# Moving a handful of vector steps, gaps and stores around in a fused attention and feed-forward kernel

## The chip, the cores and the metric

The kernel runs on one core of one Trainium2 chip. A core has five engines that run side by side, each through its own list of instructions in order: PE (TensorE, matrix products, with weight loads that overlap them), DVE (VectorE), ACT (ScalarE), POOL (GpSimd) and SP (SyncE, here only a queue that issues transfers). They meet at semaphores. The products land in PSUM, a small memory in banks which PE writes and DVE and ACT read; everything else on the chip lies in SBUF. The metric is the time of one execution on the device in microseconds (us), lower is better.

## The reference, cut to what matters

Two stages follow each other. The first is a linear attention with decay for 4 batches, 8 heads, 768 tokens and head size 64, in blocks of 64 tokens:

```python
for b in range(nb):                                  # 12 blocks of 64 tokens
    intra = einsum('bhic,bhjc->bhij', qb, kb) * Dmask
    intra = einsum('bhij,bhjd->bhid', intra, vb)
    inter = einsum('bhid,bhde->bhie', qb * lam_pow, kv_state)
    out[:, :, sl] = intra + inter
    kv_state = lam_block * kv_state + einsum('bhsd,bhse->bhde', kb * rev_pow, vb)
```

Its output, read as 3072 tokens of 512 features, goes through a feed-forward layer with an ELU:

```python
h = x @ w_in                                         # 512 -> 2048
g = where(h > 0, h, exp(minimum(h, 0)) - 1)
out = g @ w_out                                      # 2048 -> 512
```

## The kernel before, in words

**Blocks, groups, rounds.** Two batches by one block of 64 tokens make a *block* s of 128 rows; there are 24 (s = 0 to 23). Two blocks make a *group* of 256 rows; there are 12. The tile framework runs with a manual schedule: every engine's list is in the order in which the program writes the instructions, so the order of the Python text is the order of work. A string of words (`start`) writes out the first part, up to block 8 of the attention and group 2 of the feed-forward; then a loop runs *rounds* `grp` = 3 to 11, each of eight steps `u` = 0 to 7, and a written-out tail ends the program.

**One step of a round.** Step u calls `mm1_h` (L385): eight matmuls that give H(grp,u), a PSUM tile `psH` of two features blocks by 256 tokens. There are two such tiles (`bufs=2`), so H(grp,u) can start when the reader of the tile before the last has finished. Then, by step, come a *visit* to the attention (at u = 1 and 5), four matmuls of `mm2` for block 5 at four places (the list `five`), a *part* of the second product (below), small DVE and ACT work, and at the end `elu(grp,u)`, which turns H into `g` in float16.

**Two forms of the ELU.** In round 3 `mm1_e` and `mm1_g` are used: ACT reads the PSUM tile twice (exponential L395, Relu L397), which frees it, and DVE joins the two SBUF tiles (L402: both inputs in SBUF). In rounds 4 to 11 ACT makes the Relu of the negative (L429) and then its exponential from SBUF (L431), and DVE joins that with the PSUM tile itself (L432), which frees the tile.

**A visit.** `visit(s, ...)` puts out, in this order on PE, the first half of the products with the old state (L304), the scores of block s+1 (L328), the state update of block s (L320, which reads `vd` of block s), the other half with the state, the products with the scores (L313) and, for early blocks, transposes (L335). What it needs is made beforehand: `vd` of block s+1 by `decay_v` (L191, DVE, two SBUF inputs), at u = 3 and u = 6; `qs` and `sd` of block s+1 by `decay_q` (L209) and `decay_s` (L200), on DVE for early blocks and, from block 10 on, on POOL. POOL also issues all loads of q, k and v (L70), six to a block, in the same list.

**The second product.** Blocks 0 to 5 take 16 plain matmuls each (`mm2`, L452). From group 3 on a group is done by seven products of half size (`part`, L508), Strassen-like: they need sums of `g` (`g_sum`, L490) and four sums of quarters of `w_out`, the tiles `wt[1]` to `wt[4]` (`w_sum`, L478, half a tile a call). The parts go into two PSUM banks A and B; `keep` (L538, ACT) copies a bank's part out before it is written again, `add` (L542) and `c2` (L546) on DVE make the output tiles, and `store` (L527) issues two transfers for each, one for each batch, both on SP.

**Where the change touches.** In the tail the parts of group 11 use the two `psH` tiles as their banks, and the last four stores are: the first half of block 22 on SP, block 23 on SP, the second half of block 22 on ACT and SP.

Of the kernel before, what the change touches and what calls it, by code (L numbers as in the profile page):

```python
# [16 lines left out]
def kernel(  # L17
# [35 lines left out]
    def half(x):  # L53
        return slice(64 * x, 64 * x + 64)
# [365 lines left out]
    def elu(grp, u):  # L420

        psH, nb, T, name = unit[grp, 0, 2, u]
        if grp == 3:
            mm1_e(grp, 0, 2, u)
            mm1_g(grp, 0, 2, u, NF2)
            return

        r = msb.tile([128, nb, T], FP32, tag="r", bufs=4, name=f"r{name}")
        nc.scalar.activation(r[:], psH[:], AF.Relu, scale=-1.0)  # L429
        e = msb.tile([128, nb, T], FP32, tag="e", bufs=4, name=f"e{name}")  # L430
        nc.scalar.activation(e[:], r[:], AF.Exp, scale=-1.0)  # L431
        nc.vector.scalar_tensor_tensor(  # L432
            out=place(grp, 0, 2, u, 2, NF2), in0=e[:], scalar=-1.0, in1=psH[:],
            op0=ALU.add, op1=ALU.max,
        )
# [4 lines left out]
    def rows(s, r):  # L440

        b, c = where(s)
        r0 = (b + r) * S + c * L
        return out[r0 : r0 + L, :]


    def mm2(s, n0):
        if n0 == 0:
            acc[s] = M[nacc[0] % 2][:]
            nacc[0] += 1  # L450
        for n in range(n0, n0 + 4):
            nc.tensor.matmul(  # L452
                acc[s], lhsT=g_of(s, n), rhs=wo[n // 4][:, n % 4, :],
                start=(n == 0), stop=(n == NFT - 1),
            )
# [26 lines left out]
    def g_sum(grp, i):  # L482
        A = gel[grp]
        A11, A12, A21, A22 = (A[:, :, j, c * 128 : (c + 1) * 128] for c in range(2) for j in range(2))
        gs[grp, i] = msb.tile([128, NF2, 128], FP16, tag=f"s{i}", name=f"s{i}_{grp}")
        a, b = {
            1: lambda: (A21, A22), 2: lambda: (gs[grp, 1][:], A11), 3: lambda: (A11, A21),
            4: lambda: (A12, gs[grp, 2][:]),
        }[i]()
        nc.vector.tensor_tensor(  # L490
            out=gs[grp, i][:], in0=a, in1=b, op=ALU.add if i == 1 else ALU.subtract
        )
# [32 lines left out]
    def store(s, o, cols):  # L525
        for r in range(2):
            nc.sync.dma_start(out=rows(s, r)[:, cols], in_=o[half(r), cols])  # L527

    def out_tile(grp, c):
        d = res[grp]  # L530
# [10 lines left out]
        o = out_tile(grp, c)[:, cols]  # L541
        nc.vector.tensor_tensor(out=o, in0=src, in1=res[grp][kept][:], op=ALU.add)  # L542

    def c2(grp):
# [5 lines left out]
        store(2 * grp + 1, d[1], slice(0, DM))  # L550

    def consts(i):
        if i == 0:
# [42 lines left out]

    lo, hi = slice(0, HD), slice(HD, DM)

    sums = {(3, 4): 2, (4, 0): 4, (4, 3): 3}
    five = [(3, 2), (3, 5), (4, 0), (4, 2)]  # L600
    nload = 12
    for grp in range(3, NG):
        old, new = grp - 2, grp - 1
        for u in range(8):
            mm1_h(grp, 0, 2, u, NF2)
            s = 2 * grp + 2 + u // 4
            if s < NS and u % 4 == 0:

                if nload < NS:
                    load("k", nload)  # L610
                    load("q", nload)
                if nload <= NS:
                    load("v", nload - 1)
                    nload += 1
            if s < NS and u % 4 == 1:
                decay_q(s + 1, nc.vector if s < 9 else nc.gpsimd)
                decay_s(s + 1, nc.vector if s < 9 else nc.gpsimd)
                visit(
                    s, s if s < NS - NPR else None, s + 1 if s + 1 < NS else None,
                    s + 2 if s + 2 < NT else None,  # L620
                )
# [12 lines left out]
            if new >= 3 and u in (4, 5, 6, 7):
                g_sum(new, {4: 1, 5: 2, 6: 4, 7: 3}[u])
            if new >= 3 and u == 4:
                add(new, 0, lo, res[new]["A"][:, hi], "p2")
            if s + 1 < NS:
                if u % 4 == 1:
                    att_P(s + 1)  # L640
                if u % 4 == 2:
                    att_C(s + 2)
                    att_N(s)
                if u in (3, 6):
                    decay_v(s + 1, nc.vector)
# [46 lines left out]
    for r in range(2):  # L692
        (nc.scalar, nc.sync)[r].dma_start(out=rows(2 * G, r)[:, hi], in_=d[0][half(r), hi])


# [28 lines left out]
```

## Time and profile before

| | |
|---|---|
| runs shown | 214.62, 215.43 and 218.25 us; median 215.43 |
| profiled execution | 214.9 us; its span, from the first to the last instruction, 213.1 us |
| mean granted TensorE clock | 0.992 |
| PE busy | 191.2 us, 90% of the span, 3384 matmuls |
| DVE busy | 170.3 us, 80% |
| ACT busy | 141.6 us, 66% |
| POOL busy | 136.8 us, 64% |

Times within the profile are counted from the first instruction. Busy is the time in which at least one instruction of the engine runs; PE's matmuls overlap, so full rows of PE mean that matmuls follow each other without a gap, not that nothing could be quicker. A row of the timeline gives the start, the time from the first start to the last end, the line, the tile written and those read, the count and, in brackets, the idle time of the engine ahead of it with what ended it. DVE instructions that follow each other overlap by some 0.08 us, so a row of 0.68 us costs 0.60 us of the queue.

### The profile page before, as it was taken

Reading aid. Unit: us, or ns where it says so; the run is one execution under the profiler, and the core shown is the slowest. Engines: PE = TensorE matmul, PEld = TensorE weight load, DVE = VectorE, ACT = ScalarE, POOL = GpSimd, SP = SyncE. Lnnn points to the kernel's source line nnn. Section 1 sums busy time; section 2 is a strip of 40 time slices with the busy share of each in tenths; the row PEclk is TensorE's granted clock in tenths of the full one; section 3 lists DMA queues with packets and bytes.
Section 4 is the critical chain, followed back from the end, with each engine's and each line's share of the span. In section 5 each row is a group of like instructions: output and inputs, shape, how many; then the busy total and the mean of one; then the engine's idle time right before and its main releaser. Section 6 shows DMA issues by size and latency. Waiting matters only on the chain.

```text
span 213.1 us, 7908 instructions
## 1 busy us (share of the span) xinstructions
PE 191.2 (90%) x3384; PEld 158.3 (74%) x3384; DVE 170.3 (80%) x278; ACT 141.6 (66%) x265; POOL 136.8 (64%) x184
## 2 busy tenths in 40 slices
PE   0448989999999994899999999999999999999990
PEld 0347978648777763588888888888888888888880
DVE  3677895789997999897997997997979967757751
ACT  5314786724766874377868878778878788887620
POOL 8979832998999999997979979979522200000000
PEclk9999999999999999699999999999999999999999
DMA  6999999999999999997998999999923304013044
GB/s 103 142 151 157 170 201 184 180 126 163 124 140 124 116 148 105 105 105 81 130 171 78 144 164 65 137 132 119 161 42 73 80 3 101 3 24 75 3 98 98
DMA packets 98643, 24.11 MB, mean 113 GB/s; under 512 B 91312, under 2 KB 95664, under 8 KB 98608
## 3 DMA queue, kind: packets, MB, share of 16 engines
q0 software_dynamic: 78208, 13.38, 85.7%
q1 hardware_dynamic: 19120, 9.90, 25.9%
q10 hardware_dynamic: 1280, 0.33, 0.9%
q8 instruction: 26, 0.43, 0.8%
q14 instruction: 9, 0.07, 0.1%
HBM read 27.27 MB, written 6.29 MB: 157 GB/s over the span
## 4 chain that ended last, share of the span: by engine, by line
PE 80%; DVE 9%; POOL 3%; DMA 3%; ACT 1%; issue 1%; POOLq 0%; DVEq 0%
PE psH L385 37%; PE psM L508 23%; PE psM L452 9%; DVE g L402 3%; DMA wi<-in_moe_w_in_dram 3%; PE psO_None L304 2%; PE psZ L328 2%; POOL vn L70 1%; PE psHB L508 1%; PE psHA L508 1%; PE psO_None L313 1%; PE psZ L320 1%; DVE vd L191 1%; DVE wt L478 1%; DVE P L217 1%
## 5 line engine op out<-in xcount | busy, mean ns | idle before, releaser
L385 PE MATMUL psH<-xt,wi 128*128 128x256 f16 (+1 forms) x960 | 101.5, 256 | 6.8 <-DVE g L432 4.0
L385 PEld LDWEIGHTS <-wi 128*128 128x128 f16 x960 | 80.2, 100 | 18.3 <-issue 8.0
L432 DVE SCALAR_TENSOR_TENSOR g<-e,psH 128x512 f16<-128x512 f32 x64 | 43.8, 685 | 18.4 <-ACT e L431 17.8
L429 ACT ACTIVATE r<-psH 128x512 f32<-128x512 f32 x64 | 38.2, 597 | 25.7 <-PE psH L385 25.4
L431 ACT ACTIVATE e<-r 128x512 f32<-128x512 f32 x64 | 40.3, 630 | 2.0
L70 POOL DMA_DIRECT2D qn<-in_q_dram x46 | 32.3, 729 | 4.8 <-issue 4.4
L70 POOL DMA_DIRECT2D kn<-in_k_dram x46 | 32.6, 728 | 3.3 <-DMA wo<-in_moe_w_out_dram 2.5
L70 POOL DMA_DIRECT2D vn<-in_v_dram x48 | 34.2, 748 | 0.1
L395 ACT ACTIVATE e<-psH 128x512 f32<-128x512 f32 x32 | 19.2, 599 | 17.4 <-PE psH L385 17.3
L508 PEld LDWEIGHTS <-s 128*128 128x128 f16 x288 | 28.2, 98 | 3.3
L402 DVE SCALAR_TENSOR_TENSOR g<-e,r 128x512 f16<-128x512 f32 x32 | 24.4, 772 | 5.8 <-ACT r L397 5.8
L508 PE MATMUL psM<-wt,s 128*128 128x256 f16 x192 | 24.9, 273 | 0.0
L452 PE MATMUL psM<-wo,g 128*128 128x512 f16 x96 | 24.8, 390 | 0.0
L209 POOL TENSOR_TENSOR qs<-TD,powi 128x512 f16<-128x512 f16 x13 | 16.2, 1245 | 12.1 <-PE psO_None L304 12.1
L508 PEld LDWEIGHTS <-g 128*128 128x128 f16 x216 | 20.6, 98 | 2.7
L200 POOL TENSOR_TENSOR sd<-st,lamL 128x512 f32<-128x512 f16 x12 | 15.8, 1315 | 8.1 <-DVE st L264 8.1
L397 ACT ACTIVATE r<-psH 128x512 f16<-128x512 f32 x32 | 19.2, 599 | 0.0
L217 DVE TENSOR_TENSOR P<-psZ,mask 128x512 f16<-128x512 f32 x24 | 16.4, 685 | 2.5 <-PE psZ L328 2.2
L508 PE MATMUL psM<-wo,g 128*128 128x256 f16 x136 | 17.6, 273 | 0.0
L191 DVE TENSOR_TENSOR vd<-vn,rev 128x512 f16<-128x512 f16 x22 | 16.3, 739 | 0.1
L252 ACT CAST xt<-psO_None 128x512 f16<-128x512 f32 x19 | 10.9, 573 | 5.5 <-PE psO_None L313 5.5
L264 DVE TENSOR_TENSOR st<-psZ,sd 128x512 f16<-128x512 f32 x20 | 13.6, 681 | 0.9 <-PE psZ L320 0.9
(77 smaller groups left out, 209.0 us busy)
## 6 DMA issues: line engine op xcount, KB each, us to landing
out_dram<-o SPq DMA_DIRECT2D x46, 128.0 KB, 2.9
vn<-in_v_dram POOLq DMA_DIRECT2D x48, 64.0 KB, 4.5
kn<-in_k_dram POOLq DMA_DIRECT2D x46, 64.0 KB, 4.7
qn<-in_q_dram POOLq DMA_DIRECT2D x46, 64.0 KB, 3.4
wi<-in_moe_w_in_dram POOLq DMA_DIRECT2D x8, 256.0 KB, 6.0
wo<-in_moe_w_out_dram POOLq DMA_DIRECT2D x4, 512.0 KB, 11.3
kraw<-in_k_dram SPq DMA_DIRECT2D x2, 128.0 KB, 4.4
qraw<-in_q_dram ACTq DMA_DIRECT2D x2, 128.0 KB, 4.6
```

The costliest lines, as they stand in the source:

```text
L70: nc.gpsimd.dma_start(out=keep[s][half(r)], in_=src[b + r, :, c * L : (c + 1) * L, :].rearrange("h p d -> p h d"),)
L191: eng.tensor_tensor(out=st[s]["vd"][:], in0=vn[s][:], in1=rev[:].unsqueeze(2).broadcast_to([128, H, D]), op=ALU.mult,)
L217: nc.vector.tensor_tensor(out=d["P"][:].rearrange("p y j t -> p y (j t)"), in0=psS, in1=mask[:].rearrange("p y j t -> p y (j t)"), op=ALU. ...
L385: nc.tensor.matmul(psH[:, i, :], lhsT=wi[n // 4][:, kk, (n % 4) * 128 : (n % 4 + 1) * 128], rhs=xt[grp][:, kk, c0 * 128 : c0 * 128 + T], s ...
L395: nc.scalar.activation(e[:], psH[:], AF.Exp)
L397: nc.scalar.activation(r[:], psH[:], AF.Relu)
L402: nc.vector.scalar_tensor_tensor(out=place(grp, c0, nc_, n0, nb, step), in0=e[:], scalar=-1.0, in1=r[:], op0=ALU.add, op1=ALU.min,)
L429: nc.scalar.activation(r[:], psH[:], AF.Relu, scale=-1.0)
L431: nc.scalar.activation(e[:], r[:], AF.Exp, scale=-1.0)
L432: nc.vector.scalar_tensor_tensor(out=place(grp, 0, 2, u, 2, NF2), in0=e[:], scalar=-1.0, in1=psH[:], op0=ALU.add, op1=ALU.max,)
L452: nc.tensor.matmul(acc[s], lhsT=g_of(s, n), rhs=wo[n // 4][:, n % 4, :], start=(n == 0), stop=(n == NFT - 1),)
L508: nc.tensor.matmul(to, lhsT=lhsT, rhs=rhs, start=start and n == 0, stop=stop and n == NF2 - 1, skip_group_check=True,)
```

## The change

Six edits, in the program's order:

1. The two sums `wt[2]` and `wt[4]` (second halves) are made at the end of `start`, ahead of round 3, where before they stood at steps (3,4) and (4,0); that of `wt[3]` moves from step (4,3) to step (4,7).
2. Steps 6 and 7 of round 3 use the form of the ELU in which DVE reads PSUM; steps 0 to 5 keep the other.
3. In round 3, `vd` at u = 3 and u = 6 is made after that step's ELU instead of ahead of it.
4. The four pieces of block 5's second product stand at steps (3,2), (3,4), (3,6) and (4,0) instead of (3,2), (3,5), (4,0) and (4,2), and its copy and store with the last of them.
5. In round 11 the parts of group 10 stand at other steps (2, 4, 1, 5, 6, 3 at u = 1, 3, 4, 5, 6, 7), so that only part 7 is left for the tail; the copies and the sums of `g` that go with them move along, and the tail's `c2` of group 10 stands ahead of group 11's part 1.
6. The store of block 23 goes out on SP and ACT, one transfer each, instead of both on SP.

```diff
 def elu(grp, u):
-        if grp == 3:
+        if grp == 3 and u < 6:
...
-        "... A7.7.8.9 G2.1.1.8 M4.12 X7 N7 P8 Z4 C9 "
+        "... A7.7.8.9 G2.1.1.8 M4.12 X7 N7 P8 Z4 C9 B2.1 B4.1 "
...
-    sums = {(3, 4): 2, (4, 0): 4, (4, 3): 3}
-    five = [(3, 2), (3, 5), (4, 0), (4, 2)]
+    sums = {(4, 7): 3}
+    five = [(3, 2), (3, 4), (3, 6), (4, 0)]
...
-            if new >= 3 and u > 2:
-                part(new, {3: 2, 4: 1, 5: 4, 6: 5, 7: 6}[u])
+            if new >= 3:
+                at_u = {1: 2, 3: 4, 4: 1, 5: 5, 6: 6, 7: 3} if end else {3: 2, 4: 1, 5: 4, 6: 5, 7: 6}
+                if u in at_u:
+                    part(new, at_u[u])
...
-                if u in (3, 6):
+                if u in (3, 6) and grp > 3:
                     decay_v(s + 1, nc.vector)
...
             elu(grp, u)
+            if grp == 3 and u in (3, 6):
+                decay_v(s + 1, nc.vector)
...
+            if end and u == 6:
+                keep(new, "u2", res[new]["A"][:, hi], 1)
+            if end and u == 7:
+                add(new, 0, hi, res[new]["B"][:, hi], "u2")
+                store(2 * new, res[new][0], slice(0, DM))
...
-    keep(G, "u2", d["A"][:, hi], 1)
-    part(G, 3)
-    add(G, 0, hi, d["B"][:, hi], "u2")
-    store(2 * G, d[0], slice(0, DM))
     part(G, 7)
...
     g_sum(G, 1)
+    c2(G - 1)
     part(G, 1)
-    c2(G - 1)
...
-    c2(G)
+    c2(G, (nc.sync, nc.scalar))
```

More of the change, by code (lines that the diff above doesn't have):

```diff
@@ L523, in part, with store @@
         product_of(grp, i, d[bank][:, cols], first, i in (4, 2, 3, 7))
-    def store(s, o, cols):
+    def store(s, o, cols, queues=(nc.sync, nc.sync)):
         for r in range(2):
-            nc.sync.dma_start(out=rows(s, r)[:, cols], in_=o[half(r), cols])
+            queues[r].dma_start(out=rows(s, r)[:, cols], in_=o[half(r), cols])
     def out_tile(grp, c):
@@ L542, in add, with c2 @@
         nc.vector.tensor_tensor(out=o, in0=src, in1=res[grp][kept][:], op=ALU.add)
-    def c2(grp):
+    def c2(grp, queues=(nc.sync, nc.sync)):
         d = res[grp]
@@ L549, in c2 @@
         )
-        store(2 * grp + 1, d[1], slice(0, DM))
+        store(2 * grp + 1, d[1], slice(0, DM), queues)
     def consts(i):
@@ L625 @@
                 mm2(5, 4 * five.index((grp, u)))
+            end = grp == NG - 1
             if old >= 3 and u in (0, 2):
                 part(old, {0: 3, 2: 7}[u])
-            if new >= 3 and u > 2:
-                part(new, {3: 2, 4: 1, 5: 4, 6: 5, 7: 6}[u])
+            if new >= 3:
+                at_u = {1: 2, 3: 4, 4: 1, 5: 5, 6: 6, 7: 3} if end else {3: 2, 4: 1, 5: 4, 6: 5, 7: 6}
+                if u in at_u:
+                    part(new, at_u[u])
             if old >= 3 and u == 1:
@@ L633 @@
                 store(2 * old, res[old][0], slice(0, DM))
-            if new >= 3 and u in (4, 5, 6, 7):
-                g_sum(new, {4: 1, 5: 2, 6: 4, 7: 3}[u])
+            if new >= 3 and u in (4, 5, 6, 3 if end else 7):
+                g_sum(new, {4: 1, 5: 2, 6: 4}.get(u, 3))
             if new >= 3 and u == 4:
@@ L654 @@
                 keep(old, "p35", res[old]["B"][:, hi])
-            if new >= 3 and u == 3:
+            if new >= 3 and u == (1 if end else 3):
                 keep(new, "p2", res[new]["B"][:, lo])
-            if new >= 3 and u == 6:
+            if new >= 3 and u == (5 if end else 6):
                 keep(new, "c45", res[new]["B"][:])
+            if end and u == 6:
[3 more added lines that the diff above has]
+                store(2 * new, res[new][0], slice(0, DM))
             if (grp, u) == five[-1]:
@@ L688 @@
     part(G, 7)
-    c2(G)
+    c2(G, (nc.sync, nc.scalar))
     part(G, 3)
     add(G, 0, hi, HB[:, hi], "u2")
-    for r in range(2):
-        (nc.scalar, nc.sync)[r].dma_start(out=rows(2 * G, r)[:, hi], in_=d[0][half(r), hi])
+    store(2 * G, d[0], hi, (nc.scalar, nc.sync))
 _INS = ['q', 'k', 'v', 'lam', 'moe_w_in', 'moe_w_out']
```

2 rows, old and new, of the table start are left out of this document.

## The prediction

> **What bounds the kernel now.** First the page: who is busy.
>
> ```profile
> PE 191.2 (90%) x3384; PEld 158.3 (74%) x3384; DVE 170.3 (80%) x278; ACT 141.6 (66%) x265; POOL 136.8 (64%) x184
> ```
>
> PE is the bound nearly everywhere. The windows in which it isn't, at the end of round 3, and one of the later rounds for comparison (columns: busy time of PE, weight loads, DVE, ACT, POOL, then the granted clock):
>
> ```profile
> 79.92:83.33 3.41, 2.25 (x75) 1.63 (x74) 3.41 (x4) 2.65 (x5) 3.41 (x4) 1.00 1.89 123
> 83.33:86.74 3.41, 0.84 (x8) 0.75 (x8) 3.41 (x5) 0.00 (x0) 3.41 (x5) 1.00 0.76 99
> 86.74:90.16 3.42, 3.42 (x14) 1.83 (x13) 2.74 (x5) 1.81 (x3) 3.42 (x5) 0.50 1.48 94
> 100.00:120.00 20.00, 20.00 (x355) 17.51 (x354) 17.04 (x29) 16.20 (x30) 17.99 (x24) 1.00 1.35 123
> ```
>
> From 100 to 120 us PE has no gap. From 80 to 87 us DVE has none, and PE waits; then PE runs 3.41 us at half clock. So the end of round 3 is DVE's. The timeline of PE there (in brackets the idle time ahead):
>
> ```profile
> 73.86 1.03 PE L385 MATMUL psH<-xt,wi 128*128 128x256 f16 x8 [0.30 <-ACT r L397]
> 75.04 0.30 PE L320 MATMUL psZ<-vd,kn 64*64 64x64 f16 x16
> 75.50 1.04 PE L452 MATMUL psM<-wo,g 128*128 128x512 f16 x4
> 76.37 1.91 PE L385 MATMUL psH<-xt,wi 128*128 128x256 f16 x16
> 78.58 1.03 PE L385 MATMUL psH<-xt,wi 128*128 128x256 f16 x8 [0.30 <-ACT r L397]
> 85.90 1.09 PE L385 MATMUL psH<-xt,wi 128*128 128x256 f16 x8 [3.70 <-DVE g L432]
> 91.06 1.04 PE L385 MATMUL psH<-xt,wi 128*128 128x256 f16 x8
> ```
>
> These are H(3,5), visit 9's state update and a piece of block 5, H(3,6) and (3,7), H(4,0), H(4,2), H(4,4). The gap of 3.70 us is a wait for g(4,0), which frees H(4,0)'s tile. Why it came late, DVE and POOL say:
>
> ```profile
> 69.18 0.69 DVE L402 SCALAR_TENSOR_TENSOR g<-e,r 128x512 f16<-128x512 f32 x1 [1.18 <-ACT r L397]
> 73.99 0.68 DVE L191 TENSOR_TENSOR vd<-vn,rev 128x512 f16<-128x512 f16 x1
> 74.59 1.65 DVE L402 SCALAR_TENSOR_TENSOR g<-e,r 128x512 f16<-128x512 f32 x1
> 76.17 1.52 DVE L478 TENSOR_TENSOR wt<-wo,wt 128x1024 f16<-128x1024 f16 x1
> 80.01 1.62 DVE L191 TENSOR_TENSOR vd<-vn,rev 128x512 f16<-128x512 f16 x1
> 81.56 3.09 DVE L402 SCALAR_TENSOR_TENSOR g<-e,r 128x512 f16<-128x512 f32 x2
> 84.57 0.68 DVE L478 TENSOR_TENSOR wt<-wo,wt 128x1024 f16<-128x1024 f16 x1
> 85.17 0.68 DVE L432 SCALAR_TENSOR_TENSOR g<-e,psH 128x512 f16<-128x512 f32 x1
> 74.04 1.65 POOL L209 TENSOR_TENSOR qs<-T,powi 128x512 f16<-128x512 f16 x1
> 75.66 1.49 POOL L200 TENSOR_TENSOR sd<-st,lamL 128x512 f32<-128x512 f16 x1
> 81.16 1.49 POOL L209 TENSOR_TENSOR qs<-TD,powi 128x512 f16<-128x512 f16 x1
> 82.62 1.47 POOL L200 TENSOR_TENSOR sd<-st,lamL 128x512 f32<-128x512 f16 x1
> ```
>
> DVE steps of 0.68 us take 1.5 to 1.65 us where a POOL `qs` or `sd` runs: g(3,3) ends 0.55 us after `qs`, `wt` 0.55 us after `sd`, g(3,6) and g(3,7) after the next pair. DVE steps with two SBUF inputs and POOL's two steps hold each other off. (The `vd` at 80.01 us is held, too, beside POOL's loads, for a reason that I can't read.) Each hold costs 0.85 to 0.95 us of DVE's queue; five stand ahead of g(4,0).
>
> **The change, part by part.** *Sums of w_out.* wt[2] and wt[4] fall into the 1.18 us in which DVE waits ahead of g(3,0): one costs 0.60 us of the queue, the second reads the first's result and so costs about 0.7, in all up to 0.1 us too much. They leave 1.52 us (76.17) and 0.60 us (84.57) of a full queue. *g(3,6) and g(3,7)* read PSUM. Such a step is not held:
>
> ```profile
> 97.34 1.42 POOL L200 TENSOR_TENSOR sd<-st,lamL 128x512 f32<-128x512 f16 x1 [1.24 <-DVE st L264]
> 97.78 0.68 DVE L432 SCALAR_TENSOR_TENSOR g<-e,psH 128x512 f16<-128x512 f32 x1
> 98.38 0.93 DVE L490 TENSOR_TENSOR s<-g 128x1024 f16<-128x1024 f16 x1
> 99.46 0.69 DVE L432 SCALAR_TENSOR_TENSOR g<-e,psH 128x512 f16<-128x512 f32 x1 [0.15 <-ACT e L431]
> 99.72 1.04 PE L508 MATMUL psM<-wo,s 128*128 128x256 f16 x8
> 100.59 1.04 PE L385 MATMUL psH<-xt,wi 128*128 128x256 f16 x8
> ```
>
> The g at 97.78 us runs its 0.68 us beside `sd`, while the two-SBUF sum behind it is stretched to 0.93. So the two cost 1.2 us of queue in place of 3.0. The price is the tile: it is free only when DVE has read it, not after ACT. ACT's rows give the cycle:
>
> ```profile
> 79.65 0.60 ACT L429 ACTIVATE r<-psH 128x512 f32<-128x512 f32 x1
> 80.28 0.63 ACT L431 ACTIVATE e<-r 128x512 f32<-128x512 f32 x1
> ```
>
> H(4,0) began at 78.58, its Relu 1.07 us later, the exponential ends 1.26 us after that, g follows 0.04 us on, takes 0.68, and PE starts 0.05 us behind g (85.85 to 85.90): 3.10 us from a tile's first matmul to its next use, if DVE is free.
>
> [...]
>
> *Block 5's pieces, and vd behind g.* I lay the rows out in the new order. A block of eight matmuls takes 0.87 us of PE (99.72 to 100.59), a piece of block 5 the same (75.50 to 76.37), a block with visit 1.64 (73.86 to 75.50). The piece now ahead of H(3,5) covers its 0.30 us wait, and H(3,5) starts at 74.25. On DVE g(3,3) is next in line at 73.99 plus up to 0.1 us, where `vd` stood; POOL's `qs` comes at 74.04. Whoever is first holds the other; I take POOL. Then g(3,3) ends near 75.8, vd9 falls beside `sd` and is done near 77.2. Visit 9's update needs vd9 and was due at 75.43 (75.04 plus 0.39): PE idles 1.77 us, a new wait. Everything of the visit behind the update, H(3,6) and the next matmuls stand behind it.
>
> From there (DVE's four steps between vd9 and g(3,6), 2.4 us, are done before H(3,6)'s exponential): update 77.2, H(3,6) 77.66 (0.46 later, as 75.04 to 75.50), piece 78.53, H(3,7) 79.40. H(4,0) waits for H(3,6)'s tile, 77.66 + 3.10 = 80.76; piece 81.63. H(4,1) could start at 82.50, when its tile is due as well (79.40 + 3.10), but vd10 stands ahead of g(3,7) and meets `qs` at 81.16; held as at 80.01, it makes that 83.0. H(4,2) 84.64; H(4,3) waits for H(4,1)'s tile, 83.0 + 3.10 = 86.10; the part 86.97; H(4,4) 87.84, where it was 91.06: **3.2 us less**. In this the half clock is gone (the longest gap is 1.77 us).
>
> Bounds: with g(3,3) ahead of `qs`, vd9 ends at 76.24 as the step at 74.59 did, g(3,4) is held by `sd` as `wt` was (to 77.69), three more steps bring g(3,6) at 79.4 and H(4,0) at 80.1; vd10 is past before 81.16, H(4,1) at 81.9, H(4,3) 85.0 and H(4,4) 86.7: 4.4 us less. With vd9 held a full `sd` (77.7) and vd10 twice, H(4,4) comes 1.5 us later than taken: 1.7 us less.
>
> *Block 5's copy and store* move up, too. On ACT the copy stands ahead of H(4,1)'s Relu, which is late itself: nothing. On SP the store now stands ahead of block 13's transposes:
>
> ```profile
> 82.68 1.19 SPq L239 DMA_TRANSPOSE TD<-kn  x1
> 94.86 1.24 POOL L209 TENSOR_TENSOR qs<-TD,powi 128x512 f16<-128x512 f16 x1
> ```
>
> They slip some 2 us, and the `qs` that reads them ran 12 us later: nothing.
>
> *Rounds 4 and 5.* PE is now some 3 us early; POOL is not, for it was busy 17.99 of 20 us and none of its steps moves up. Its holds fall on other DVE steps until it has caught up. wt[3], gone from 89.86, now stands between the sum at 98.38 and g(4,7). That g had 0.15 us of idle time ahead and ended at 100.15, H(5,1) wanted the tile at 100.59: 0.59 us to spare in all. Unheld, wt[3] costs 0.60: nothing. Held once 0.9 more, with the sum held as well 1.5. I take **0.7 us back**, bounds 0 and 1.5. From round 6 on PE is dense again.
>
> *Tail.*
>
> ```profile
> 188.87 0.35 ACT L538 COPY p<-psM 128x256 f32<-128x256 f32 x1
> 189.73 1.03 PE L385 MATMUL psH<-xt,wi 128*128 128x256 f16 x8 [0.32 <-DVE g L432]
> 207.05 2.38 SPq L527 DMA_DIRECT2D out_dram<-o  x4
> 208.36 0.42 DVE L542 TENSOR_TENSOR o<-psHB,u 128x256 f32<-128x256 f32 x1 [0.19 <-PE psHB L508]
> 208.82 0.55 ACTq L693 DMA_DIRECT2D out_dram<-o  x1
> 209.53 0.76 SPq L693 DMA_DIRECT2D out_dram<-o  x1
> ```
>
> Part 2 now fills the wait ahead of H(11,2), since the copy that must empty its bank ends at 189.22, before PE comes to it (189.73 less 0.32 is 189.41): **0.3 us less**. The number of parts is the same. One part fewer stands between H(11,7) and group 11's part 1 (1.74 us instead of 2.62); g(11,7) is needed only by that part's last matmul, 0.76 us further, so 0.87 + 1.74 + 0.76 = 3.4 covers the 3.10: nothing. The last store waited 0.71 us on SP for the four ahead (209.53 against 208.82). With one of them on ACT, idle then, SP is free at about 208.85, and the short form takes 0.55, not 0.76: up to 0.85 us, 0.3 if both queues slow each other; I take **0.7 us less**.
>
> Sum: 3.2 - 0.7 + 0.3 + 0.7 = 3.5 us, from the profiled execution's 214.9: **211.4 us**. That execution lies between the runs of 214.62 and 215.43; the median, 215.43, is half a microsecond above it, so I say 211.5. A change under 2% (4.3 us) is about what a measurement of this kernel can't tell from none.
>
> **Rivals.** *POOL loses the race* at 74 us (its start and g(3,3)'s lie within 0.1 us): 4.4 less, 0.3 back, 1.0 in the tail: 209.8. *The holds eat it*: lower bound 1.7, 1.5 back, 1.0 in the tail: 213.7; for it speaks that DVE's two-SBUF steps only change places under the same POOL steps. *The new form waits where the old didn't* (slower): the tile of H(3,6) now hangs on DVE's queue. If g(3,6) still ended at 83.20, as in the pair at 81.56, PE would stand from 79 to 83.25 ahead of H(4,0), long enough for the half clock (1.7 us); H(4,1) 84.99, H(4,3) 88.1, H(4,4) 89.8, with the clock 91.5, 0.45 us late; with 1.5 back and 1.0 in the tail 215.9. It decides from a g(3,6) over 2.5 us behind the 80.0 taken here; against it speaks that 1.5 us of `wt` no longer stands ahead. *The reading of PSUM is held as well*: 1.9 us more, 213.4; the row at 97.78 speaks against it.
>
> *The clock trips anyway*: a window 25% busy tripped it (0.84 of 3.41), one 66% busy (2.25) did not; the longest gap here leaves about half. It would cost 1.7 us: 213.2. [...]
>
> **How the numbers follow.** Forecast (210.6 to 212.6) 0.50; race lost by POOL 0.24; holds, PSUM held or clock, which give 212.6 to 214.2, 0.22; slower 0.04. The range leaves out the slower rival and the outer ends: 209.5 to 214.1. Faster by over 2% (under 210.6, from the profiled time) is the race's 0.24 and a little of the forecast: 0.27; within 2% 0.71; slower by over 2% 0.02.
>
> **What would show it.** No `wt` step between 70 and 90 us; g(3,6) and g(3,7) at 0.68 us; no half clock; a PE wait for `vd` in visit 9 and short ones ahead of H(4,0) and H(4,3); H(4,4) near 87.8; holds on the sums of rounds 4 and 5; no gap ahead of H(11,2); both last stores issued within 0.1 us. The forecast is wrong if the sums don't fit the 1.18 us, or if POOL's holds spread over all later rounds.

## The result, and the profile after

The changed kernel takes 214.21 us (median of 20 runs, 211.99 to 215.40). The kernel before, run beside it, takes 216.06 us (median of 20, 214.62 to 219.15). The ratio is 0.990, with a 95% interval of 0.986 to 0.993: **1.0% or some 2.2 us faster**; the medians differ by 1.85 us. (Ratios here leave out executions more than 1.5% above their kernel's fastest, medians take in all, so the two need not agree.) The profiled execution took 214.37 us, its span is 212.6 us. I had forecast 211.5 us, in a range of 209.5 to 214.1.

Windows of the changed kernel (columns as in the prediction: PE, weight loads, DVE, ACT, POOL, clock):

```profile
76.00:80.00 4.00, 2.86 (x83) 2.24 (x82) 4.00 (x5) 2.19 (x5) 4.00 (x6) 1.00 1.87 150
84.00:88.00 4.00, 3.41 (x87) 2.57 (x86) 2.92 (x5) 3.56 (x7) 4.00 (x7) 1.00 0.53 74
92.00:100.00 8.00, 6.19 (x114) 5.42 (x114) 8.00 (x11) 4.63 (x8) 8.00 (x11) 1.00 1.66 103
100.00:120.00 20.00, 20.00 (x355) 17.39 (x354) 17.48 (x30) 16.05 (x29) 16.80 (x21) 1.00 1.24 118
```

The half clock of round 3 is gone, and from 100 us on PE is dense as before. But from 92 to 100 us, where PE had no gap before, it now works 6.19 of 8 us, with DVE and POOL busy throughout.

The comparisons below use one measure: the time from H(3,0), where round 3 begins on PE, to a later tile. It leaves out the first 67 to 70 us, which differ from execution to execution. (How far the rest differs, too, is told below.) First, H(3,0), H(4,4) and H(5,2) in PE's timeline of the changed kernel:

```profile
68.27 1.36 PE L385 MATMUL psH<-xt,wi 128*128 128x256 f16 x11
...
89.17 1.04 PE L385 MATMUL psH<-xt,wi 128*128 128x256 f16 x8
...
102.51 1.05 PE L385 MATMUL psH<-xt,wi 128*128 128x256 f16 x8
```

and H(3,0) and H(5,2) of the kernel before (its H(4,4), at 91.06, stands in the prediction):

```profile
66.98 1.25 PE L385 MATMUL psH<-xt,wi 128*128 128x256 f16 x10
...
102.25 1.05 PE L385 MATMUL psH<-xt,wi 128*128 128x256 f16 x8
```

H(4,4) comes 20.90 us behind H(3,0), where it was 24.08: 3.18 us less. H(5,2) comes 34.24 us behind it, where it was 35.27: 1.03 us less. So round 3 gave what was forecast, and within one more round two thirds of it were gone: H(4,4) to H(5,2) takes 13.34 us instead of 11.19.

Where it went is read from PE's waits. These are the waits for another engine that its timeline lists from 73 to 100 us (those over 0.15 us):

```profile
78.43 0.32 PE L320 MATMUL psZ<-vd,kn 64*64 64x64 f16 x16 [1.14 <-DVE vd L191]
82.19 1.03 PE L385 MATMUL psH<-xt,wi 128*128 128x256 f16 x8 [0.54 <-DVE g L432]
84.30 1.03 PE L385 MATMUL psH<-xt,wi 128*128 128x256 f16 x8 [0.21 <-DVE g L432]
87.41 1.05 PE L385 MATMUL psH<-xt,wi 128*128 128x256 f16 x8 [0.38 <-DVE g L432]
99.05 1.03 PE L385 MATMUL psH<-xt,wi 128*128 128x256 f16 x8 [1.81 <-DVE g L432]
```

The first four are the wait for `vd` in visit 9 and those of H(4,0), H(4,1) and H(4,3): 2.27 us, in place of the 3.70 and the half clock of before. The fifth is new: H(5,0) waits 1.81 us for its tile, which g(4,6) frees. DVE's timeline shows both ends of the story, first round 3, then the stretch ahead of 99.05:

```profile
69.00 1.41 DVE L478 TENSOR_TENSOR wt<-wo,wt 128x1024 f16<-128x1024 f16 x2
...
74.67 0.68 DVE L402 SCALAR_TENSOR_TENSOR g<-e,r 128x512 f16<-128x512 f32 x1
75.52 1.41 DVE L402 SCALAR_TENSOR_TENSOR g<-e,r 128x512 f16<-128x512 f32 x1 [0.16 <-ACT r L397]
76.85 1.52 DVE L191 TENSOR_TENSOR vd<-vn,rev 128x512 f16<-128x512 f16 x1
...
79.50 1.44 DVE L402 SCALAR_TENSOR_TENSOR g<-e,r 128x512 f16<-128x512 f32 x1
...
81.46 0.67 DVE L432 SCALAR_TENSOR_TENSOR g<-e,psH 128x512 f16<-128x512 f32 x1
82.06 1.59 DVE L191 TENSOR_TENSOR vd<-vn,rev 128x512 f16<-128x512 f16 x1
83.58 0.67 DVE L432 SCALAR_TENSOR_TENSOR g<-e,psH 128x512 f16<-128x512 f32 x1
...
94.49 1.34 DVE L490 TENSOR_TENSOR s<-g,s 128x1024 f16<-128x1024 f16 x1
95.75 0.68 DVE L264 TENSOR_TENSOR st<-psZ,sd 128x512 f16<-128x512 f32 x1
96.35 2.04 DVE L191 TENSOR_TENSOR vd<-vn,rev 128x512 f16<-128x512 f16 x1
98.32 0.68 DVE L432 SCALAR_TENSOR_TENSOR g<-e,psH 128x512 f16<-128x512 f32 x1
98.92 0.68 DVE L490 TENSOR_TENSOR s<-g 128x1024 f16<-128x1024 f16 x1
99.52 0.68 DVE L478 TENSOR_TENSOR wt<-wo,wo 128x1024 f16<-128x1024 f16 x1
```

and POOL's:

```profile
74.68 1.70 POOL L209 TENSOR_TENSOR qs<-T,powi 128x512 f16<-128x512 f16 x1
76.34 1.48 POOL L200 TENSOR_TENSOR sd<-st,lamL 128x512 f32<-128x512 f16 x1
...
81.84 1.25 POOL L209 TENSOR_TENSOR qs<-TD,powi 128x512 f16<-128x512 f16 x1
...
88.59 1.25 POOL L209 TENSOR_TENSOR qs<-TD,powi 128x512 f16<-128x512 f16 x1
...
93.96 1.41 POOL L70 DMA_DIRECT2D vn<-in_v_dram  x2
95.31 1.53 POOL L209 TENSOR_TENSOR qs<-TD,powi 128x512 f16<-128x512 f16 x1
96.82 1.03 POOL L200 TENSOR_TENSOR sd<-st,lamL 128x512 f32<-128x512 f16 x1
```

The two ELU steps that read PSUM (81.46, 83.58) run unheld, as forecast, in 0.67 us each; the one of 74.67, both inputs in SBUF and not held, took 0.68. But ahead of g(4,6) stand the sum `s4` (94.49), 0.66 us too long beside POOL's loads, and `vd` of block 12 (96.35; the one that step (4,6) makes), which is held first by `qs` and then, without a break, by `sd`: 2.04 us where 0.68 would do. Together these are 2.0 us, against 1.81 us of PE's wait. The kernel before had the same `vd` here:

```profile
97.18 0.68 DVE L191 TENSOR_TENSOR vd<-vn,rev 128x512 f16<-128x512 f16 x1
```

It went free, since POOL stood idle: `qs` ended at 96.10 and `sd` waited 1.24 us for `st` (the row at 97.34 us in the prediction). `st` and then `vd` stand in this order on DVE, so when POOL has to wait for `st`, `vd` arrives with it. In the changed kernel PE and DVE are early, `st` is there before `qs` is done, `sd` follows `qs` at once, and `vd` finds POOL busy. POOL itself has its own pace, 6.75 and 6.72 us from `qs` to `qs` (81.84, 88.59, 95.31). Counted from H(3,0), the `qs` of 95.31 us, that of block 13, moved up by 0.8 us (27.88 before, 27.04 now), where PE moved up by 3.2.

The rows also show which of two steps was held. At 74.67 DVE came first: g(3,2) took its 0.68 us, and the `qs` that began 0.01 us behind it 1.70, where those of 81.84 and 88.59 took 1.25. (In the kernel before, the `vd` of 73.99 took 0.68 us and the `qs` of 74.04 took 1.65.) Next POOL came first: g(3,3) at 75.52, 0.84 us behind the `qs` of 74.68, ended 0.55 us after it. And the `st` of 95.75, which reads one of its two inputs from PSUM, took its 0.68 us beside the `qs` of 95.31.

### The profile page after: what moved, and what is told of

Its sections match the earlier page's. It is cut to its first block, busy times and chain, and to the rows that moved or that the text cites. A ratio compares the mean times of both kernels' runs of the same rounds, so it can differ in the third digit from the quotient of the medians.

```text
span 212.6 us, 7909 instructions
## 1 busy us (share of the span) xinstructions
PE 190.4 (90%) x3384; PEld 157.4 (74%) x3384; DVE 171.0 (80%) x278; ACT 141.8 (67%) x265; POOL 136.5 (64%) x184
## 4 chain that ended last, share of the span: by engine, by line
PE 54%; POOL 20%; DMA 16%; issue 4%; DVE 2%; ACT 1%; POOLq 0%; DVEq 0%
PE psH L385 25%; PE psM L508 22%; DMA wo<-in_moe_w_out_dram 9%; POOL qn L70 6%; POOL kn L70 5%; POOL vn L70 5%; DMA kn<-in_k_dram 3%; DMA vn<-in_v_dram 3%; POOL wi L88 2%; PE psO_None L304 2%; DMA qn<-in_q_dram 1%; DVE g L432 1%; PE psHB L508 1%; PE psHA L508 1%; PE psO_None L313 1%
## 5 line engine op out<-in xcount | busy, mean ns | idle before, releaser
L432 DVE SCALAR_TENSOR_TENSOR g<-e,psH 128x512 f16<-128x512 f32 x66 | 45.1, 684 | 17.5 <-ACT e L431 17.0
L429 ACT ACTIVATE r<-psH 128x512 f32<-128x512 f32 x66 | 39.4, 597 | 24.1 <-PE psH L385 24.0
L431 ACT ACTIVATE e<-r 128x512 f32<-128x512 f32 x66 | 41.6, 630 | 2.1
L395 ACT ACTIVATE e<-psH 128x512 f32<-128x512 f32 x30 | 18.0, 599 | 17.8 <-PE psH L385 17.8
L402 DVE SCALAR_TENSOR_TENSOR g<-e,r 128x512 f16<-128x512 f32 x30 | 21.8, 735 | 4.5 <-ACT r L397 4.5
L452 PE MATMUL psM<-wo,g 128*128 128x512 f16 x96 | 23.9, 380 | 0.0
L191 DVE TENSOR_TENSOR vd<-vn,rev 128x512 f16<-128x512 f16 x22 | 18.9, 858 | 1.2 <-DMA vn<-in_v_dram 1.2
L397 ACT ACTIVATE r<-psH 128x512 f16<-128x512 f32 x30 | 18.0, 599 | 0.0
## 6 DMA issues: line engine op xcount, KB each, us to landing
wo<-in_moe_w_out_dram POOLq DMA_DIRECT2D x4, 512.0 KB, 10.2
```

The lines of the kernel that those rows point to most:

```text
L191: eng.tensor_tensor(out=st[s]["vd"][:], in0=vn[s][:], in1=rev[:].unsqueeze(2).broadcast_to([128, H, D]), op=ALU.mult,)
L395: nc.scalar.activation(e[:], psH[:], AF.Exp)
L397: nc.scalar.activation(r[:], psH[:], AF.Relu)
L402: nc.vector.scalar_tensor_tensor(out=place(grp, c0, nc_, n0, nb, step), in0=e[:], scalar=-1.0, in1=r[:], op0=ALU.add, op1=ALU.min,)
L432: nc.vector.scalar_tensor_tensor(out=place(grp, 0, 2, u, 2, NF2), in0=e[:], scalar=-1.0, in1=psH[:], op0=ALU.add, op1=ALU.max,)
L452: nc.tensor.matmul(acc[s], lhsT=g_of(s, n), rhs=wo[n // 4][:, n % 4, :], start=(n == 0), stop=(n == NFT - 1),)
```

## The experiments

The theory that the expectations carry is that one cause, POOL's `qs` and `sd` against DVE's steps with two SBUF inputs, made the loss in round 3 and takes back the gain in rounds 4 and 5. Its rivals are named in each.

**Halves of the change.** The kernel before with edits 1 to 4:

```diff
-        if grp == 3:
+        if grp == 3 and u < 6:
...
-        "... X7 N7 P8 Z4 C9 "
+        "... X7 N7 P8 Z4 C9 B2.1 B4.1 "
...
-    sums = {(3, 4): 2, (4, 0): 4, (4, 3): 3}
-    five = [(3, 2), (3, 5), (4, 0), (4, 2)]
+    sums = {(4, 7): 3}
+    five = [(3, 2), (3, 4), (3, 6), (4, 0)]
...
-                if u in (3, 6):
+                if u in (3, 6) and grp > 3:
...
+            if grp == 3 and u in (3, 6):
+                decay_v(s + 1, nc.vector)
```

> The kernel before with edits 1 to 4 alone (sums, ELU form, vd, block 5), the tail as before. Theory A (POOL's holds take back what round 3 gains): the gain is 3.2 us at H(4,4) less some 2 us in rounds 4 and 5, so 1 to 1.5 us faster than before; a gap of 1 to 2 us ahead of H(5,0) or H(5,1). Theory B (round 3 keeps its gain, and the loss in the one profile was an accident of that run): 3 us faster, no gap over 0.7 us after 90 us.

Measured: 214.71 us against 215.61, ratio 0.994 (0.990 to 0.998). H(4,4) comes 20.28 us behind H(3,0), H(5,2) 33.29: 1.82 us of the gain are given back in between, and in the same place as in the whole change. PE and DVE of this kernel there:

```profile
98.62 1.03 PE L385 MATMUL psH<-xt,wi 128*128 128x256 f16 x8 [1.51 <-DVE g L432]
```

```profile
95.56 2.41 DVE L191 TENSOR_TENSOR vd<-vn,rev 128x512 f16<-128x512 f16 x1
```

`vd` takes 2.41 us, the sum and `wt[3]` that I had suspected 0.68 each. Theory A came out, Theory B did not. The kernel before with edits 5 and 6 alone (two of its lines, the steps of the parts and the queues of the last store):

```diff
+                at_u = {1: 2, 3: 4, 4: 1, 5: 5, 6: 6, 7: 3} if end else {3: 2, 4: 1, 5: 4, 6: 5, 7: 6}
...
-    c2(G)
+    c2(G, (nc.sync, nc.scalar))
```

> The kernel before with edits 5 and 6 alone (parts of group 10 in round 11, last stores on two queues). Both theories: 0.3 us from the gap ahead of H(11,2) and 0.4 to 0.7 us from the stores, 0.7 to 1.0 us faster than before. If the stores only shift the landing (rival), 0.3 us.

Measured: ratio 0.992 (0.987 to 0.997); but the medians of all runs, 215.51 and 215.61 us, hardly differ. From H(11,0) on its trace is the changed kernel's: 8.91 us from H(11,7) to the end of PE (9.79 before), 4.52 us from there to the end of the span (4.84 before). From H(5,2) to the end of the span it takes 110.05 us and the changed kernel 110.07, where the kernel before and the one with edits 1 to 4 both take 110.86. So by the traces the tail is worth 0.8 us, with and without edits 1 to 4. Rounds 3 to 5 are worth some 1.3 us by the runs of the kernel with edits 1 to 4 (0.6% of 215.6), 1.0 us at H(5,2) by the profile of the whole change and 2.0 us by that of edits 1 to 4.

These four profiles also tell how far a single one can be trusted. Up to the tail the whole change and edits 1 to 4 alone are the same code, yet H(4,4) comes at 20.90 and 20.28 us, H(5,2) at 34.24 and 33.29. The kernel before and the one with the tail alone are the same code there, too: 24.08 and 23.50, 35.27 and 34.69. So a difference of less than 1 us between two single profiles says nothing.

**POOL's steps taken away.** From block 10 on no `qs` or `sd` is made on POOL; the visits read block 9's tiles again. In the kernel before, and then the same in the changed one:

```diff
 def decay_s(s, eng):
+        if s >= 10:
+            st[s]["sd"] = st[9]["sd"]
+            return
...
 def decay_q(s, eng):
+        if s >= 10:
+            st[s]["qs"] = st[9]["qs"]
+            return
```

> The kernel before without POOL's qs and sd (from block 10 on the tiles of block 9 are read again, so the decay of the later blocks is left out); the loads stay. Theory A (holds by POOL's two steps make the stall of round 3): no DVE step over 1.2 us, the 3.7 us gap ahead of H(4,2) and the half clock gone, H(3,0) to H(5,2) 35.3 us becomes 30 to 31, the kernel 4 to 5 us faster than before. Theory B (DVE has simply too much to do there): a gap of 1 to 2 us stays, 2 to 3 us faster.

> The changed kernel without POOL's qs and sd, in the same way. Theory A: the waits for vd9 and ahead of H(5,0) are gone, H(3,0) to H(5,2) takes 30 us as in the kernel before without them, and the two differ by the tail alone, 0.8 us. Theory B: the change keeps 2 us or more of its own over the other kernel without these steps.

Measured: 211.18 us (ratio 0.976, 0.970 to 0.982) and 211.33 us (0.974, 0.967 to 0.981). Four runs of each don't tell the two kernels apart without POOL's steps. H(4,4) comes 19.66 and 19.30 us behind H(3,0), H(5,2) 30.85 and 30.49, and from there to the end of the span it takes 111.12 and 110.35 us, the tail's 0.8. These are the windows of the kernel before without the steps, the same 10 us as in the prediction (PE, weight loads, DVE, ACT, POOL, clock), where PE had 2.25, 0.84 and, at half clock, 3.42 us (round 3 begins 1.7 us later here, at 68.72):

```profile
79.92:83.33 3.41, 3.11 (x26) 2.25 (x24) 2.71 (x5) 3.05 (x6) 3.41 (x6) 1.00 2.25 154
83.33:86.74 3.41, 3.41 (x87) 2.53 (x85) 2.83 (x5) 2.87 (x6) 2.47 (x4) 1.00 1.92 137
86.74:90.16 3.42, 3.33 (x32) 2.84 (x30) 3.09 (x5) 2.88 (x7) 3.42 (x6) 1.00 1.48 153
```

And PE's waits for another engine from 72 to 102 us in the changed kernel without them (line numbers are 6 higher), with the `vd` of block 12 on DVE:

```profile
82.31 1.03 PE L391 MATMUL psH<-xt,wi 128*128 128x256 f16 x8 [0.33 <-DVE g L438]
87.16 1.05 PE L391 MATMUL psH<-xt,wi 128*128 128x256 f16 x8 [0.41 <-DVE g L438]
```

```profile
94.88 0.68 DVE L191 TENSOR_TENSOR vd<-vn,rev 128x512 f16<-128x512 f16 x1
```

No half clock, no wait for `vd` in visit 9, none of 1.81 us ahead of H(5,0). The 3.70 us of before, the half clock and the new waits of after hang on POOL's two steps. With them go the holds and also anything that waits for `qs` or `sd`; but from 66 us on the traces of before and after list no wait of another engine for POOL, so it is the holds. What is left of round 3 are the waits ahead of H(4,0) and H(4,3), 0.7 us. The kernel before without the steps waits 0.30 us each ahead of H(3,5) and H(4,0) instead, so neither form of the ELU comes out ahead.

**Edits undone one at a time in the changed kernel.** Edit 2, that is, steps 6 and 7 of round 3 read SBUF again:

```diff
-        if grp == 3 and u < 6:
+        if grp == 3:
```

> The changed kernel with steps 6 and 7 of round 3 in the old form (both ELU inputs of DVE in SBUF), all other edits kept. If the reading of PSUM is worth what the prediction said, g(3,6) and g(3,7) can be held again: 1 to 2 us slower than the changed kernel. Rival: the tiles come free earlier, from ACT, which pays for the holds: within 0.5 us of the changed kernel, 1.5 to 2.5 us faster than before.

Edit 1, the sums back in rounds 3 and 4:

```diff
-        "... C9 B2.1 B4.1 "
+        "... C9 "
-    sums = {(4, 7): 3}
+    sums = {(3, 4): 2, (4, 0): 4, (4, 3): 3}
```

> The changed kernel with edit 1 undone: wt[2] at step (3,4), wt[4] at (4,0), wt[3] at (4,3) again, all else as changed. Theory A (the holds set the time, and round 4 takes back what round 3 gains): two sums, one of them held, come back into round 3 and delay g(4,0) and g(4,1), 1 to 1.5 us more at H(4,4), but round 4 then gives less back: from H(3,0) to H(5,2) 34 to 35.5 us, where the changed kernel took 34.24 and the kernel before 35.26. Theory C (edit 1 alone is the gain): 35.3 us or more, as before.

Edit 3, `vd` ahead of the ELU again at (3,3) and (3,6):

```diff
-                if u in (3, 6) and grp > 3:
+                if u in (3, 6):
...
-            if grp == 3 and u in (3, 6):
-                decay_v(s + 1, nc.vector)
```

> The changed kernel with edit 3 undone: vd9 and vd10 ahead of g(3,3) and g(3,6) again. The wait for vd9 in visit 9 (1.14 us in the changed kernel) goes; g(3,6) comes later behind vd10 and the gap ahead of H(4,0) grows from 0.5 to 1.5 to 2 us. Both nearly cancel: H(3,0) to H(4,4) 20 to 21.5 us, where the changed kernel took 20.89, and to H(5,2) 33.5 to 34.5 us.

Edit 4, block 5's pieces back:

```diff
-    five = [(3, 2), (3, 4), (3, 6), (4, 0)]
+    five = [(3, 2), (3, 5), (4, 0), (4, 2)]
```

> The changed kernel with edit 4 undone: block 5's pieces at (3,2), (3,5), (4,0), (4,2) again. The pieces no longer cover the waits for tiles in round 3: 0.3 us ahead of H(3,5) and 0.5 to 0.9 us more ahead of H(4,0), but a piece fills the wait ahead of H(4,3). H(3,0) to H(4,4) 21 to 21.8 us (changed kernel 20.89), to H(5,2) 34 to 35 us.

Measured, beside the whole change (H times are behind H(3,0), in the profiled execution):

| undone | median us | ratio to before (95%) | H(4,4) | H(5,2) | H(4,4) to H(5,2) | H(4,4) to POOL's `qs` of block 13 |
|---|---|---|---|---|---|---|
| nothing | 214.21 | 0.990 (0.986 to 0.993) | 20.90 | 34.24 | 13.34 | 6.14 |
| edit 1 (sums) | 213.95 | 0.992 (0.989 to 0.996) | 21.14 | 32.61 | 11.47 | 4.18 |
| edit 2 (ELU) | 213.97 | 0.994 (0.990 to 0.999) | 20.62 | 34.44 | 13.82 | 6.46 |
| edit 3 (`vd`) | 213.54 | 0.988 (0.984 to 0.992) | 22.80 | 34.08 | 11.28 | 3.93 |
| edit 4 (pieces) | 214.31 | 0.996 (0.993 to 0.999) | 21.70 | 33.94 | 12.24 | 5.35 |

No single one of the first three is worth anything that these runs can measure. For edit 4 the two intervals only just overlap; it may be worth half a per cent.

The expectations fared as follows. Without edit 2, g(3,7) is held again (1.52 us), but the loss of 1 to 2 us didn't come; the times lie by the changed kernel, as the rival had it. Without edit 1, H(4,4) comes 0.24 us later, not 1 to 1.5, and H(5,2) lies ahead of the 34 to 35.5 expected. Without edit 3, H(4,4) lies outside 20 to 21.5: the wait ahead of H(4,0) grew to 2.59 us, and the clock was at half from 84.31 to 87.72 us. (That profile isn't typical of its kernel. One window of 3.41 us at half clock takes 0.008 off a mean clock over 213 us, and 8 of its 10 runs have 0.996 or more.) Without edit 4, H(4,4) is in its range, and H(5,2) just ahead of its own.

The last two columns say why so little is left of each. The `qs` of block 13 is the POOL step beside which `vd` of block 12 stands. In the kernel before and in the one with the tail alone it begins 3.80 us behind H(4,4), and H(4,4) to H(5,2) takes 11.19 us. The earlier PE is against that `qs`, the longer this stretch takes. In all eight kernels that have all of POOL's pairs and keep `vd` of block 12 ahead of g(4,6), H(5,2) follows that `qs` by 6.9 to 7.4 us, wherever H(4,4) was. So H(5,2) goes with POOL's queue and not with what PE gained; this is read from eight profiles, and moving that `qs` alone was not tried.

With edit 1 undone POOL itself is early (`qs` of block 13 at 25.32 us behind H(3,0), 27.04 in the changed kernel), and PE meets it again as in the kernel before. DVE and POOL of that kernel:

```profile
97.42 0.68 DVE L264 TENSOR_TENSOR st<-psZ,sd 128x512 f16<-128x512 f32 x1
98.02 0.67 DVE L191 TENSOR_TENSOR vd<-vn,rev 128x512 f16<-128x512 f16 x1
```

```profile
95.69 1.24 POOL L209 TENSOR_TENSOR qs<-TD,powi 128x512 f16<-128x512 f16 x1
98.17 1.42 POOL L200 TENSOR_TENSOR sd<-st,lamL 128x512 f32<-128x512 f16 x1 [1.24 <-DVE st L264]
```

POOL waits for `st`, `vd` slips in between `qs` and `sd` at 0.67 us, and H(5,0) doesn't wait. But a free `vd` is not enough. With edit 2 undone POOL waits for `st` just as long (1.24 us) and `vd` goes free, yet H(5,0) waits 1.73 us, for here the sum `s4` ahead of both is held:

```profile
96.35 2.63 DVE L490 TENSOR_TENSOR s<-g,s 128x1024 f16<-128x1024 f16 x1
...
99.50 0.68 DVE L191 TENSOR_TENSOR vd<-vn,rev 128x512 f16<-128x512 f16 x1
```

What is gained in round 3 beyond that point, the next visit takes back, by whichever step is in the way.

**Versions that go after the give-back.** In the changed kernel `vd` of block 12 behind g(4,6):

```diff
-                if u in (3, 6) and grp > 3:
+                if u in (3, 6) and grp > 3 and (grp, u) != (4, 6):
...
-            if grp == 3 and u in (3, 6):
+            if (grp, u) in ((3, 3), (3, 6), (4, 6)):
                 decay_v(s + 1, nc.vector)
```

> The changed kernel with vd of block 12 made behind g(4,6) instead of ahead of it. Theory A: the gap of 1.8 us ahead of H(5,0) goes to under 0.7, for g(4,6) no longer waits for the held vd; what is held now comes ahead of g(4,7) and costs up to 1 us ahead of H(5,1): 0.5 to 1.5 us faster than the changed kernel. Rival (the holds only move): the same time as the changed kernel within 0.3 us.

Measured: 212.78 us against 216.35, ratio 0.984 (0.979 to 0.989). H(5,0) doesn't wait; the next tile does, for `vd` is still held, only later (PE, then DVE):

```profile
98.87 1.03 PE L385 MATMUL psH<-xt,wi 128*128 128x256 f16 x8 [0.98 <-DVE g L432]
```

```profile
95.53 1.48 DVE L191 TENSOR_TENSOR vd<-vn,rev 128x512 f16<-128x512 f16 x1
```

H(4,4) to H(5,2) takes 12.46 us: in this profile 0.9 of the 2.15 us are back. Next, `qs` and `sd` of block 10 on DVE, so that POOL has one pair less:

```diff
-                decay_q(s + 1, nc.vector if s < 9 else nc.gpsimd)
-                decay_s(s + 1, nc.vector if s < 9 else nc.gpsimd)
+                decay_q(s + 1, nc.vector if s < 10 else nc.gpsimd)
+                decay_s(s + 1, nc.vector if s < 10 else nc.gpsimd)
```

> The changed kernel with qs and sd of block 10 made by DVE (0.60 us of its queue each) in place of POOL, so that POOL is 2.7 us ahead from 76 us on and has no step beside vd9. Theory A: the wait for vd9 in visit 9 goes from 1.1 us to under 0.4, POOL's holds of rounds 4 and 5 come back to the place they had before, no gap over 0.7 us ahead of H(5,0): 1.5 to 2.5 us faster than the changed kernel, 3.5 to 5 us faster than before. Theory B: DVE has 1.2 us more to do in its fullest stretch: 0 to 1 us slower than the changed kernel.

Measured: 211.97 us against 215.61, ratio 0.986 (0.981 to 0.992). Visit 9 no longer waits, H(4,4) comes at 19.20. H(5,2) comes at 31.71, 2.5 us ahead of the changed kernel's; by the two ratios only some 0.7 us of that show, less than the 1.5 to 2.5 expected. H(5,1) waits 1.16 us, and here it is the sum and `wt[3]` that are held, the place that the prediction had named:

```profile
95.33 1.21 DVE L490 TENSOR_TENSOR s<-g 128x1024 f16<-128x1024 f16 x1
96.47 1.52 DVE L478 TENSOR_TENSOR wt<-wo,wo 128x1024 f16<-128x1024 f16 x1
```

So `wt[3]` one step on as well:

```diff
-    sums = {(4, 7): 3}
+    sums = {(5, 0): 3}
```

> The changed kernel with qs and sd of block 10 on DVE and the sum wt[3] at step (5,0), where DVE waits for ACT anyway, instead of (4,7). Theory A: the gap of 1.2 us ahead of H(5,2), which the first of the two alone left, goes to under 0.3 us; 0.5 to 1.2 us faster than that kernel, 2 to 3.5 us faster than the changed one. Rival (POOL's holds find other steps): no faster than with the first alone.

Measured: 211.54 us against 216.35, ratio 0.978 (0.973 to 0.984); PE's wait ahead of H(5,1) is 0.70 us, not under 0.3, with the sum ahead of it held 2.48 us by both POOL steps in turn. Last, that sum (`g_sum` 3) behind g at step 7 in all rounds but the last:

```diff
-            if new >= 3 and u in (4, 5, 6, 3 if end else 7):
+            if new >= 3 and u in ((3, 4, 5, 6) if end else (4, 5, 6)):
...
+            if new >= 3 and u == 7 and not end:
+                g_sum(new, 3)
```

> The kernel of e8 with the sum s3 of g (step 7 of each round) made behind that step's g instead of ahead of it. Theory A: the hold of 2.5 us that s3 met there no longer delays g(4,7), the gap of 0.7 us ahead of H(5,2) goes to under 0.2 us: 0.3 to 0.7 us faster than e8, H(3,0) to H(5,2) 30.5 us. Rival (the hold moves on to g(5,0) behind it): as e8 within 0.3 us.

Measured: 210.70 us against 215.72, ratio 0.978 (0.973 to 0.982), the fastest median, though not to be told from the version ahead of it, as the rival had it; H(5,2) comes at 31.95, not 30.5. The hold has moved on once more, back to `vd` of block 12, here behind loads and `qs`, and H(5,0) waits 1.46 us (DVE, then PE):

```profile
94.18 2.79 DVE L191 TENSOR_TENSOR vd<-vn,rev 128x512 f16<-128x512 f16 x1
```

```profile
97.62 1.03 PE L385 MATMUL psH<-xt,wi 128*128 128x256 f16 x8 [1.46 <-DVE g L432]
```

All four have lower medians than both kernels, and the intervals of the last two lie clear of the changed kernel's. With POOL's pair of block 10 gone, H(5,2) comes at 31.3 to 32.0 us, some 1 us behind the 30.5 and 30.85 that are left without any POOL step.

## Why the prediction was wrong

The sum, term by term, from the two profiled executions:

| term | predicted us | measured us |
|---|---|---|
| start, up to H(3,0) | 0 | +1.29 |
| round 3, up to H(4,4) | -3.2 | -3.18 |
| H(4,4) to H(5,2) ("rounds 4 and 5") | +0.7 | +2.15 |
| H(5,2) to H(11,0) | 0 | 0.0 |
| H(11,0) to the end of PE | -0.3 | -0.48 |
| end of PE to the end of the span (last stores) | -0.7 | -0.30 |
| sum | -3.5 | -0.5 |

Without the first row, which is the scatter of the start, the measured sum is -1.8 us, and the medians differ by 1.85.

**Right.** What bounds round 3, and that POOL would be first at `qs`: 74.68 against 75.52. The walk through the rows held to 0.2 us in this profile. Counted from H(3,0), vd9 was forecast done at 10.2 and was at 10.10, H(4,0) forecast at 13.8 and at 13.92, H(4,1) 16.0 and 16.03, H(4,3) 19.1 and 19.14, H(4,4) 20.86 and 20.90. That it fits so closely is partly luck: the same code gave 20.28 with edits 1 to 4 alone, and the pairs of profiles put the gain of round 3 between 2.6 and 3.8 us. The two sums took 1.41 us (69.00) and did fit ahead of g(3,0), which follows H(3,0) by 2.20 us before and 2.19 after. No half clock in the profile, no `wt` from 70.5 to 99 us, g(3,6) and g(3,7) at 0.67 us, no gap ahead of H(11,2). Of the rivals "POOL loses the race", "the PSUM read is held" and "the clock trips anyway" none came true. "The holds eat it" (213.7) came nearest, but by a smaller gain in round 3 (1.7) and less given back (1.5) than there was.

**Wrong: the term "Rounds 4 and 5, 0.7 us back".** The mechanism was the one named, POOL's holds on a PE that is early; the term was mis-sized, 2.15 us in this profile and 1.82 with edits 1 to 4 alone, both outside its bounds of 0 and 1.5. I looked for it at step (4,7), where `wt[3]` was added, and bounded it by one hold of the sum and one of `wt[3]`. It fell one step earlier, on `vd` of block 12 and `s4` ahead of g(4,6), which the change doesn't touch. Two things were left out of the bounds. A step can be held by `qs` and by `sd` in turn (2.04 and 2.41 us where 1.65 was the longest row of before). And the free passage of `vd` in the kernel before rested on POOL waiting 1.24 us for `st`; the row at 97.34 us showed that wait, and I quoted it for another purpose. With PE 3.2 us early that wait is gone, and the pair closes up. This was 1.45 us. The term asked what one added step would cost, where it should have asked how far POOL's `qs` of block 13 moves up: 0.8 us, nearly all of the 1.0 us that were left at H(5,2).

**Wrong: the base.** The sum started from a profiled execution of 214.9 us, whose round 3 began at 66.98 us. In the other 13 profiles of this case it began at 67.11 to 70.37, 68.9 on average; those whose first part is that of the kernel before gave 68.18, 68.72 and 70.37 (the last with 3.41 us at half clock from 62.76 us on), so the two added sums aren't needed to explain it. The median of 20 runs of the kernel before is 216.06, that of the three runs shown was 215.43, and I went only 0.1 us of that way. From 216.06 the same sum gives 212.6; with 2.15 us in place of 0.7 it gives 214.0, where 214.21 was measured. Of the 1.2 us between 214.9 and 216.06, 0.5 could be read from the three runs shown; the rest they couldn't show.

**The tail** was forecast 0.2 us too good. SP and ACT were done with their last issues within 0.3 us of each other, and the one on SP ended 0.90 us behind DVE's last addition, as these two rows of the changed kernel show, first SP with its two last stores, then DVE:

```profile
208.03 1.43 SPq L527 DMA_DIRECT2D out_dram<-o  x2
```

```profile
208.14 0.42 DVE L542 TENSOR_TENSOR o<-psHB,u 128x256 f32<-128x256 f32 x1 [0.19 <-PE psHB L508]
```

Before it was 1.51 us (210.29 against 208.78). Of these 0.61 us only 0.30 reach the end of the span, the lower bound given: what follows the issue got longer by the rest. Why that is stays open.

The 0.27 given to "faster by over 2%" hung on POOL losing its race; by the table of undone edits a larger gain in round 3 would probably have been handed back, too, in good part. The race itself wasn't met as drawn: `qs` came 0.01 us behind g(3,2) and 0.84 us ahead of g(3,3), not within 0.1 us of g(3,3).

## What to carry to other kernels

Where steps of two engines hold each other up, as DVE's and POOL's did here (`vd` 2.04 us in place of 0.68, `qs` 1.70 in place of 1.25), a gain on one of them can be lost at the next place where the two meet, as 2.15 of 3.18 us were here: follow the early engine to the first steps of the other that didn't move up, and ask of each row there that went free why it was free. A short wait of an engine that seems to bound nothing (POOL's 1.24 us for `st`) can be what keeps that place open. Start a sum from the median of the runs, or say how far the profiled execution's own early part is from it, before a difference of 1% is forecast.

## What the runs showed that I had not expected

Steps of DVE with two SBUF inputs were held also where POOL only issued loads: g(3,5) at 79.50 took 1.44 us and `s4` at 94.49 1.34 us, with no `qs` or `sd` of POOL running beside the first and none beginning beside the second until 0.82 us into it. The kernel with edits 1 to 4 alone has such a step at 1.15 us. In the two kernels without POOL's steps the loads are issued as before, and not one DVE step in rounds 3 to 11 takes over 0.70 us. So it isn't the issuing of loads by itself; what POOL's two steps have to do with these holds stays open.

POOL's pace is not PE's. While nothing stops it, POOL goes from `qs` to `qs` in 6.7 us, six loads and two steps, and PE takes 7.3 us for a visit in the later rounds (73.1 us from H(6,0) to H(11,0), ten visits). So it catches up 0.6 us a visit, and from H(5,0) on no DVE step of the changed kernel takes over 0.84 us. Taking one pair from POOL, at block 10, brought H(5,2) from 34.24 to 31.71 us behind H(3,0), where the change's own edits in round 3 had brought it from 35.27 to 34.24.

The half clock came without an idle window, and the changed kernel came close to it. The granted clock falls to 0.50 for 3.41 us within four of the profiles. In the 3.41 us just ahead PE was busy 0.84 us in the kernel before, 0.85 with edits 5 and 6 alone, 0.82 with edit 3 undone and, in its first part, 1.36 with edit 1 undone. In the trace of the kernel before the clock is recorded from 21.89 us on and falls at 86.74, 19 times 3.413 us later. In that of the changed kernel it is recorded from 21.96 us on; counted from there in steps of 3.41 us, the emptiest window ahead of the tail holds the new wait ahead of H(5,0), with 1.60 us, and the clock stays full behind it. The kernel with edit 1 undone, then the changed kernel (columns as before):

```profile
59.34:62.75 3.41, 1.36 (x47) 1.22 (x48) 2.19 (x4) 2.05 (x5) 3.25 (x5) 1.00 1.79 143
62.75:66.17 3.42, 3.42 (x97) 1.87 (x83) 3.42 (x7) 0.59 (x1) 3.42 (x6) 0.50 1.68 145
```

```profile
97.05:100.46 3.41, 1.60 (x15) 1.28 (x14) 3.41 (x5) 0.95 (x2) 3.41 (x5) 1.00 1.26 70
```

Counted in the same way in all 14 profiles, every window up to 40% busy is followed by the half clock (at the end of the program, too), and none with 46% or more is. Nor does every execution of the kernel before trip it: of its 69 runs beside the experiments, 24 have a mean clock of 0.994 or more, which leaves no room for such a window. The gain of 3.2 us in round 3 is counted from a profile that has one.
